# Turning a token tile round by a float32 product instead of by DMA, and placing the transform's groups anew

## The chip, the cores and the metric

The program runs on one core of a Trainium2 chip. The metric is the device time of one execution in microseconds (us), as the median of several runs. Besides, one execution was recorded by the hardware profiler; the rows below are from that one. The engines are TensorE (PE, with its weight loads as PEld), VectorE (DVE), ScalarE (ACT), GpSimd (POOL) and SyncE, whose queue (SP) issues most of the DMA transfers. Each engine works through its own instructions in order and waits on semaphores for the others. A tile is a buffer of 128 partitions; a bank is a tile of 128x512 float32 values in PSUM, the memory into which TensorE writes.

## The reference, cut to what matters

Two batches of 768 tokens go through three layers: a retention attention, then a Fourier mixing with an MLP, then a second MLP. The change lies in the Fourier mixing of the second batch.

```python
X = np.fft.fft(x, axis=1)          # along 768 tokens
X = np.fft.fft(X, axis=2)          # along 512 features
u = x + np.real(X)
un = (u - mean(u)) / np.sqrt(var(u) + 1e-6)
x = u + np.maximum(un @ w_ch1, 0.0) @ w_ch2
# and then the second MLP layer on that x
```

## The kernel before

**What is computed where.** A batch `b` is held as six token tiles `U[b][0..5]` of 128x512. The token transform uses the symmetry of cosine and sine: tile `m` and tile `3 + m`, which holds the mirrored tokens, are added and subtracted, and the same is done along the features. `fold_half` does this for one `m` (lines 528 to 545) and leaves a folded tile `f` (`folds[b, m][2]`). For the second batch (`b` = 1) the fold goes one step further: the folded tile of `m` = 2, with its token order reversed, is added to and subtracted from the folded tile of `m` = 0. The reversed tile is called `turned`, the two results `radd` and `rsub` (lines 588 to 594). Each is split into a float16 part and a float16 remainder (`fadd`, `fsub`, made by `pair_of_rows`: a cast on ACT, then a subtraction on POOL, lines 561 to 565). `dft1_two` (line 612) then makes the five groups of the token transform, banks `ps_d_2`, `ps_d_3`, `ps_d_4`, `ps_d_0`, `ps_d_1`, from `fm` (the fold of `m` = 1), `fadd` and `fsub`. `dft2_*` makes the feature transform from them, and the layer norm and `unT` (the transposed input of the MLP) follow.

**How the tile is turned.** `fold_turn` (lines 569 to 583) writes `f` to DRAM (`turned_d`), copies it there row by row in reversed order (`turned_e`), and loads it back as `turned`. Row 0 stays zero. That makes three DMA transfers, one behind the other on the SP queue.

**What runs meanwhile.** The MLP of the first batch (blocks 0 and 1) and later of the second (blocks 2 and 3) is a long list of steps. Step `n` does the up product of one slice `f` of the hidden layer (line 843, bank `ps_h`, 12 matmuls 128x384; from block 2 on also in a form with fewer products, line 952), its ReLU on ACT and the remainder on DVE (lines 857 and 858), and the down product of the slice of three steps before (line 1003, banks `ps_y`, 9 matmuls 128x512). At the end of a block DVE adds the three banks `ps_y` to `u` (line 1109, the drain), which frees them for the next block.

**What sets the order.** `put(n, task)` hangs the second batch's work into step `n` (lines 1453 to 1468). The tile framework then orders each engine's instructions by these priorities and by a timeline that it simulates itself, so the order on an engine is fixed before the run. `fold_turn` stands at step 20, `fold_mid` and `fold_both` at 22, the five groups at 22.5, 23, 23.5, 24 and 24.5. Banks come from three rings: `at` (three, for attention, the weights' conversion, the transform), `dn` (three, for `ps_y`) and `up` (two, for `ps_h`).

Of the kernel before, what the change touches and what calls it, by code (L numbers as in the profile page):

```python
# [11 lines left out]
F32 = mybir.dt.float32  # L12
# [7 lines left out]
P = 128  # L20
B, H, S, D = 2, 8, 768, 64
DM, DF = 512, 2048
# [29 lines left out]
EARLY0, GATEN, B1, SPC, DS, DC, DFO, DD, D1S, D2S, AO, YA, NR, NE, LN1, L1, L2, F01, F02, TL, R1, R2, SE, PR1, LAG, UB, FB, NW, MQ, SPL = 11, 8, 6, 2.0, 2.0, 5, 1.0, 0.5, 0.5, 1.0, "aba", "aa", 2, 0, 3, 2.5, 2.5, 16, 4, 3, 1.5, 2, "dddd_dppp", 0, 3, 3, 13, 11, 1, 3  # L52
# [22 lines left out]
def split16(a):  # L75
    hi = a.astype(np.float16)
    lo = (a - hi.astype(np.float64)).astype(np.float16)
    return hi, lo


def shape_tables():
    t = np.arange(TB)
    s = np.arange(NS)
    ang = 2.0 * np.pi * ((t[:, None] * s[None, :]) % S) / S
    cs = np.cos(ang) * TS
    sn = np.sin(ang) * TS
    d = np.arange(P)
    dd = np.arange(ND)
    cd = np.cos(2.0 * np.pi * ((d[:, None] * dd[None, :]) % DM) / DM) * TS
    dse, dso = d[:, None] * dd[None, 2:-1:2], (d[:, None] + 1) * dd[None, 1::2]  # L90
    sd = np.sin(2.0 * np.pi * (np.concatenate([dso, dse], 1) % DM) / DM) * TS
    sd[P - 1, :P] *= 0.5

    def lay(a, n):
        parts = [x.reshape(n, P, -1).transpose(1, 0, 2) for x in split16(a)]
        return np.ascontiguousarray(np.stack(parts, 1))

    def full(a, n):
        return np.ascontiguousarray(a.astype(np.float32).reshape(n, P, -1).transpose(1, 0, 2))

    even, odd = np.arange(0, DM, 2), np.arange(1, DM, 2)
    wide = np.stack([np.cos(2.0 * np.pi * (d[:, None] * even % DM) / DM), np.cos(2.0 * np.pi * (d[:, None] * odd % DM) / DM),
                     -np.sin(2.0 * np.pi * (d[:, None] * even % DM) / DM), -np.sin(2.0 * np.pi * ((d[:, None] + 1) * odd % DM) / DM)], 1) * TS
    wide[0, 2] = np.where(even % 4, -0.5, 0.5) * TS
    wide[P - 1, 3] *= 0.5
    so = np.concatenate([np.arange(0, NT, 2), np.arange(1, NT, 2)])
    tc = np.cos(2.0 * np.pi * (t[:2 * P, None] * so % S) / S) * TS
    ss = so[so < TB]
    ts = np.sin(2.0 * np.pi * (t[:2 * P, None] * ss % S) / S) * TS
    ts[0] = np.sin(2.0 * np.pi * (2 * P * ss % S) / S) * TS  # L110
    r3 = np.round(2.0 * np.cos(2.0 * np.pi * (2 * P * so % S) / S)) / 2
    cr4 = np.stack([np.where(so % 2, -2.0, 0.0)] * 2 + [r3] * 2) * TS

    def two(a, n):
        return np.ascontiguousarray(np.stack([x.reshape(2, P, n).transpose(1, 0, 2) for x in split16(a)], 1))

    n = np.arange(P)
    expo = np.zeros((P, H + 8 + P), np.float32)
    expo[:, :H] = n[:, None]
    expo[:, H:H + 4] = P  # L120
    for i, m in enumerate((n < D, n >= D, n > 0, n == 0)):
        expo[:, H + 4 + i] = m
    expo[:, H + 8:] = np.eye(P)
    return {
        "cs2": two(tc, NT),
        "sn2": two(ts, TB),
        "cr4": cr4.astype(np.float16),
        "cs": lay(cs, 3),
        "sn": lay(sn[:, :TB], 3),
        "cd": lay(np.concatenate([cd[:, ::2], cd[:, 1::2]], 1), 1)[:, :, 0],  # L130
        "sd": lay(sd, 1)[:, :, 0],
        "cr": ((np.where(s % 2, -1.0, 1.0) - 1.0) * TS).astype(np.float16)[None],
        "dr": np.tile(np.where(dd[::2] % 4, -0.5, 0.5) * TS, (2, 1)).astype(np.float16),
        "cs32": full(cs, 3),
        "sn32": full(sn[:, :TB], 3),
        "wide": wide.astype(np.float32),
        "expo": expo,
    }
# [3 lines left out]
def tile_retention_fourier_mlp(ctx: ExitStack, tc: tile.TileContext, a: dict, out: bass.AP):  # L142
    nc = tc.nc
    pe, act, dve, pool, sp = nc.tensor, nc.scalar, nc.vector, nc.gpsimd, nc.sync

    const = ctx.enter_context(tc.tile_pool(name="const", bufs=1))
# [10 lines left out]
    dram = ctx.enter_context(tc.tile_pool(name="dram", bufs=1, space=DRAM))  # L157
# [5 lines left out]
    def bank(which, name):  # L163
        return banks[which].tile([P, 512], F32, tag=which, name=name)

    def f32t(name, spare=None):
        if spare is not None:
            return wpool.tile([P, 512], F32, tag=f"w2_{spare}", name=name)
        return fp.tile([P, 512], F32, tag="f", name=name)
# [12 lines left out]
    man.__enter__()  # L182
    lamb = const.tile([P, H], F32, name="lamb")
    sp.dma_start(lamb, a["lam"].partition_broadcast(P))
    expo = const.tile([P, H + 8 + P], F32, name="expo")
    act.dma_start(expo, a["expo"])
    upper, lower, nonzero, zero = (expo[:, H + 4 + i:H + 5 + i] for i in range(4))
    ident = expo[:, H + 8:]

    loaded = {}  # L190

# [93 lines left out]
    def run(steps):  # L285
        for t in steps:
            pass
        return t
# [237 lines left out]
    folds = {}  # L526
# [29 lines left out]
    def fold_two(m):  # L556
        run(fold_half(1, m, 1, pool))
        run(fold_half(1, m, 0))
        return folds[1, m][2]

    def pair_of_rows(f, name):
        t = hl(name)
        act.copy(t[:, 0], f)
        pool.tensor_tensor(t[:, 1], f, t[:, 0], op=ALU.subtract)
        return t

    turned = {}

    def fold_turn():
        f = fold_two(2)  # L570
        t = f32t("r256").bitcast(F16)[0:1].rearrange("p (two n) -> p two n", two=2)[:, :, :ND]
        act.copy(t[:, 0], f[0:1, :ND])
        pool.tensor_tensor(t[:, 1], f[0:1, :ND], t[:, 0], op=ALU.subtract)
        sp.dma_start(rows4[1][2:4], t)
        z = turned["f"] = f32t("turned")
        pool.memset(z[0:1], 0.0)
        d, e = (dram.tile([P, DM], F32, name=f"turned_{x}") for x in "de")
        sp.dma_start(d, f)
        x_, y_ = d[:], e[:]
        halves_of = [[DM // 2, 2], [DM, P - 1], [1, DM // 2]]  # L580
        sp.dma_start(bass.AP(y_.tensor, y_.offset + DM, halves_of),
                     bass.AP(x_.tensor, x_.offset + (P - 1) * DM, [[DM // 2, 2], [-DM, P - 1], [1, DM // 2]]))
        sp.dma_start(z[1:P], e[1:P])

    def fold_mid():
        fhl[1, 1] = pair_of_rows(fold_two(1), "fm1")

    def fold_both():
        f, z = fold_two(0), turned["f"]
        act.copy(f[0:1, ND:], folds[1, 2][2][0:1, ND:])  # L590
        for nm, op in (("add", ALU.add), ("sub", ALU.subtract)):
            r = f32t(f"r{nm}1")
            dve.tensor_tensor(r, f, z, op=op)
            fhl[1, nm] = pair_of_rows(r, f"f{nm}1")
# [17 lines left out]
    def dft1_two(g, bk):  # L612
        c0, w, tn, _ = GRP[g]
        cos = tn == "cs"
        n = NT // 2 if cos else HB
        t = tab[tn + "2"]
        ps = bank(bk["d"], f"ps_d1_{g}")
        todo = [(1, slice(0, 2 * n), 1), ("add" if cos else "sub", slice(0, n), 0), ("sub" if cos else "add", slice(n, 2 * n), 0)]
        if w > 1:
            for nm, o, m in todo:  # L620
                for i, (x, y) in enumerate(PASS):
                    pe.matmul(ps[:w, o], fhl[1, nm][:, x, c0:c0 + w], t[:, y, m, o], start=nm == 1 and i == 0,
                              stop=not cos and nm == "add" and i == 2, skip_group_check=True)
        else:
            for y in range(2):
                for nm, o, m in todo:
                    pe.matmul(ps[:2 - y, o], fhl[1, nm][:, :2 - y, c0], t[:, y, m, o], start=nm == 1 and y == 0, stop=False,
                              skip_group_check=True)
        if cos:
            pe.matmul(ps[:w, :2 * n], rows4[1][:, c0:c0 + w], tab["cr4"], start=False, stop=True, skip_group_check=True)  # L630
        w = max(w, 2)
        t = cst[1, g] = csp.tile([P, 2, NT], F16, tag=f"cs{g}", name=f"cst1_{g}")
        hi, lo = (t[:w, x, :2 * n].rearrange("p (i e) -> p e i", e=2) for x in range(2))
        z = ps[:w, :2 * n].rearrange("p (e i) -> p e i", e=2)
        act.activation(hi, z, AF.Copy, scale=CS)
        dve.scalar_tensor_tensor(lo, z, CS, hi, op0=ALU.mult, op1=ALU.subtract)
# [682 lines left out]
    bk1 = {"a": "at", "s": "at", "i": "at", "o": "at", "st": "at", "d": "at", "l": "at", "p": "at"}  # L1319
# [110 lines left out]
    def put(n, task):  # L1430
        bg.setdefault(max(int(n), 0), []).append((n, len(bg), task))
# [26 lines left out]
    n = t + DC + DFO  # L1458
# [2 lines left out]
    put(n, fold_both)  # L1461
    n += DD
    for i, g in enumerate((2, 3, 4, 0, 1)):
        put(n + i * D1S, lambda g=g: dft1_two(g, bk1))
    n += 4 * D1S + 1
    for j in range(3):
        put(n + j * D2S, lambda j=j: (run(dft2_q(1, j, bk1)), run(sub_sin(1, j)), dft2_x(1, j), ln_a(0, 2, j)))
# [99 lines left out]
```

## Time and profile before

| what | value |
|---|---|
| median of 3 runs | 589.98 us (589.07 to 590.15) |
| the profiled execution | 588.64 us, span 586.9 us |
| PE busy | 561.4 us (96% of the span) |
| DVE, POOL, ACT busy | 403.9, 335.5, 302.7 us |
| mean granted TensorE clock | 0.994 |

The span is the time from the first to the last instruction in the record; the execution's own time is 1.7 us longer. PE is busy nearly throughout, so what counts is where it isn't, and what it waits for there. [...]

### The profile page before, as it was taken

What the parts mean: (1) busy time and instruction counts of PE and PEld (TensorE: products, weight loads), DVE (VectorE), ACT (ScalarE), POOL (GpSimd) and SP (SyncE); (2) the same over time, 40 slices, a digit from 0 to 9 for tenths busy, and PEclk for the clock granted to TensorE, in tenths of its full rate; (3) what the DMA queues carried; (4) which work ended last, traced back from release to release, by engine and by line L of the source; (5) the groups of instructions that cost most, each with busy time, mean ns of one, the idle gap of its engine ahead of it and who ended that gap; (6) DMA issues with size and microseconds to landing.
All of it is one profiled execution on the core that took longest, in us unless ns stands there. A gap on an engine that the chain in (4) does not pass through costs nothing.

```text
span 586.9 us, 12192 instructions
## 1 busy us (share of the span) xinstructions
PE 561.4 (96%) x4700; PEld 384.5 (66%) x4700; DVE 403.9 (69%) x917; ACT 302.7 (52%) x621; POOL 335.5 (57%) x355
## 2 busy tenths in 40 slices
PE   7979999999995999989999899999999999999997
PEld 4746555566552554666677677776777778878885
DVE  6897896787864447888687866557656665756544
ACT  4867888733232232645688788954243454322320
POOL 7826599976442353655367678764096676223511
PEclk9999999999997999999999999999999999999999
DMA  8997089950010010244265443510120125002101
GB/s 282 407 412 278 23 274 252 330 182 3 1 43 12 1 36 20 58 111 152 73 166 181 144 162 115 167 27 1 55 55 1 18 88 59 1 1 75 37 1 55
DMA packets 47417, 63.92 MB, mean 109 GB/s; under 512 B 26236, under 2 KB 29183, under 8 KB 47358
## 3 DMA queue, kind: packets, MB, share of 16 engines
q1 hardware_dynamic: 46542, 62.92, 34.6%
q8 instruction: 37, 0.61, 0.4%
q10 hardware_dynamic: 816, 0.21, 0.2%
q14 instruction: 22, 0.18, 0.1%
HBM read 52.63 MB, written 6.81 MB: 101 GB/s over the span
## 4 chain that ended last, share of the span: by engine, by line
PE 62%; DVE 13%; ACT 8%; POOL 6%; DMA 6%; issue 5%; SPq 0%; DVEq 0%; POOLq 0%; ACTq 0%
PE ps_y L1003 25%; PE ps L952 21%; PE ps_h L843 5%; DVE wr L876 2%; DMA turned<-turned_e 2%; PE ps_y L1050 2%; POOL m L393 1%; DMA turned_e<-turned_d 1%; PE ps_a L1050 1%; PE ps_b L1050 1%; POOL w L343 1%; PE ps_s L381 1%; ACT top L324 1%; ACT w L341 1%; DMA ws<-in_w 1%
## 5 line engine op out<-in xcount | busy, mean ns | idle before, releaser
L1003 PE MATMUL ps_y<-w,h 128*128 128x512 f16 (+1 forms) x1026 | 249.4, 378 | 2.7 <-DVE h L989 1.6
L1003 PEld LDWEIGHTS <-h 128*128 128x128 f16 x1032 | 98.0, 98 | 89.5 <-ACT h L988 2.7
L952 PEld LDWEIGHTS <-sw 128*128 128x128 f16 x1104 | 94.6, 98 | 21.7 <-issue 3.3
L952 PE MATMUL ps<-th,sw 128*128 128x192 f16 x756 | 86.0, 246 | 2.1 <-DVE s L969 1.2
L343 POOL TENSOR_TENSOR w<-wf,w 128x512 f16<-128x512 f32 x58 | 66.9, 1160 | 32.3 <-ACT w L341 32.2
L952 PEld LDWEIGHTS <-w 128*128 128x128 f16 x828 | 70.9, 98 | 11.0 <-issue 0.8
L843 PE MATMUL ps_h<-unT,w 128*128 128x384 f16 x396 | 72.8, 328 | 1.8 <-DVE h L858 1.7
L952 PE MATMUL ps<-unT,w 128*128 128x192 f16 x552 | 61.6, 246 | 0.0
L843 PEld LDWEIGHTS <-w 128*128 128x128 f16 x396 | 38.0, 98 | 30.7 <-issue 3.2
L888 POOL TENSOR_TENSOR sw<-ws,sw 128x512 f16<-128x512 f32 x32 | 36.9, 1167 | 18.4 <-ACT sw L887 18.3
L341 ACT CAST w<-wf 128x512 f16<-128x512 f32 x58 | 35.1, 611 | 10.1 <-DVE wf L328 7.2
L1238 ACT ACTIVATE h<-ps 128x384 f16<-128x384 f32 x44 | 21.7, 496 | 34.6 <-DVE ps L1245 30.0
L917 POOL TENSOR_TENSOR th<-ts,th 128x384 f16<-128x384 f32 x22 | 20.2, 936 | 27.1 <-ACT th L916 27.1
L318 DVE SCALAR_TENSOR_TENSOR wf<-ws,ps_w 128x512 int32<-128x512 int32 x34 | 23.2, 684 | 17.1 <-ACT ps_w L316 6.7
L393 POOL TENSOR_TENSOR m<-m,m 128x512 f16<-128x512 f32 x24 | 31.6, 1332 | 5.6 <-ACT m L391 3.6
L785 POOL TENSOR_TENSOR rs<-rs,neghalf 128x1 f32<-128x1 f32 x24 | 13.5, 567 | 34.8 <-DVE rs L783 34.8
L1267 POOL TENSOR_TENSOR hh<-s,hh 128x256 f16<-128x256 f32 x22 | 14.4, 677 | 32.9 <-ACT hh L1266 30.9
L806 POOL TENSOR_TENSOR uns<-un,uns 128x512 f16<-128x512 f32 x21 | 25.4, 1207 | 13.5 <-ACT uns L805 13.5
L988 ACT ACTIVATE h<-ps 128x384 f16<-128x384 f32 x48 | 22.4, 487 | 20.5 <-DVE ps L982 18.6
L989 DVE SCALAR_TENSOR_TENSOR h<-ps,h 128x384 f16<-128x384 f32 x48 | 25.4, 553 | 10.6 <-ACT h L988 10.0
L857 ACT ACTIVATE h<-ps_h 128x384 f16<-128x384 f32 x36 | 17.1, 482 | 25.7 <-PE ps_h L843 25.7
L952 PE MATMUL ps<-unT,sw 128*128 128x192 f16 x276 | 30.3, 246 | 0.0
(248 smaller groups left out, 1031.5 us busy)
## 6 DMA issues: line engine op xcount, KB each, us to landing
ws<-in_w SPq DMA_DIRECT2D x25, 511.8 KB, 6.3
ws<-in_w2b SPq DMA_DIRECT2D x16, 511.8 KB, 4.3
ws<-in_w1b SPq DMA_DIRECT2D x16, 511.8 KB, 3.9
kt<-in_kt SPq DMA_DIRECT2D x12, 256.0 KB, 3.6
qt<-in_qt SPq DMA_DIRECT2D x12, 256.0 KB, 4.9
v<-in_v SPq DMA_DIRECT2D x12, 256.0 KB
k<-in_k SPq DMA_DIRECT2D x12, 256.0 KB, 5.0
pre<-in_w SPq DMA_DIRECT2D x4, 511.8 KB, 6.9
```

The costliest lines, as they stand in the source:

```text
L318: dve.scalar_tensor_tensor(ti, raw[:, :, 0], 13, part.bitcast(I32), op0=ALU.logical_shift_right, op1=ALU.bitwise_or)
L341: act.copy(hi, t)
L343: gate["lo"] = pool.tensor_tensor(lo, t, hi, op=ALU.subtract)
L393: pool.tensor_tensor(t[:, 1], m32, t[:, 0], op=ALU.subtract)
L806: pool.tensor_tensor(s_[:, 1], un, s_[:, 0], op=ALU.subtract)
L843: pe.matmul(ps, w[:, i, k, fo:fo + P], x[:, j, k, :], start=n == 0, stop=n == 11)
L888: pool.tensor_tensor(lo, z, hi, op=ALU.subtract)
L952: pe.matmul(ps, lhs, rhs, start=start and n == 0, stop=n == 5, skip_group_check=True)
L988: gate["relu"] = act.activation(hi, z, AF.Relu)
L989: dve.scalar_tensor_tensor(lo, z, 0.0, hi, op0=ALU.max, op1=ALU.subtract)
L1003: pe.matmul(ps, h[:, x, j * P:(j + 1) * P], w[:, y, c], start=f == first and n == 0, stop=f == NF - 1 and n == 2, skip_group_check=True)
L1050: pe.matmul(ps[:, c], lhs[:, x], rhs[:, y], start=start == 1 and n == 0 and p == 0, stop=n == 2, skip_group_check=True)
```

## The change

The tile is no longer turned by DMA. `fold_turn` makes a 128x128 tile `turning` on POOL: the identity of `expo` read from its last column backwards, with one added zero column. `fold_both` multiplies it with `f` in one float32 product into a bank of the `at` ring (`ps_turned`), and DVE reads that bank for `radd` and `rsub`. The groups are put at `n + 1 + i * D1S / 2`, which is 23.5, 23.75, 24, 24.25 and 24.5.

```diff
-    expo = np.zeros((P, H + 8 + P), np.float32)
+    expo = np.zeros((P, H + 8 + P + 1), np.float32)
...
-    expo[:, H + 8:] = np.eye(P)
+    expo[:, H + 8:-1] = np.eye(P)
...
-        z = turned["f"] = f32t("turned")
-        pool.memset(z[0:1], 0.0)
-        d, e = (dram.tile([P, DM], F32, name=f"turned_{x}") for x in "de")
-        sp.dma_start(d, f)
-        x_, y_ = d[:], e[:]
-        halves_of = [[DM // 2, 2], [DM, P - 1], [1, DM // 2]]
-        sp.dma_start(bass.AP(y_.tensor, y_.offset + DM, halves_of),
-                     bass.AP(x_.tensor, x_.offset + (P - 1) * DM, [[DM // 2, 2], [-DM, P - 1], [1, DM // 2]]))
-        sp.dma_start(z[1:P], e[1:P])
+        turned["p"] = f32t("turning")[:, :P]
+        pool.tensor_copy(turned["p"], expo[:, H + 8 + P:H + 8:-1])
...
     def fold_both():
-        f, z = fold_two(0), turned["f"]
+        z = bank(bk1["d"], "ps_turned")
+        pe.matmul(z, turned["p"], folds[1, 2][2], start=True, stop=True)
+        f = fold_two(0)
...
-        put(n + i * D1S, lambda g=g: dft1_two(g, bk1))
+        put(n + 1 + i * D1S / 2, lambda g=g: dft1_two(g, bk1))
```

Lines behind the changed function stand five lower in the changed kernel (line 1003 there is 998, 858 is 853, 1109 is 1104). The order of instructions differs from PE's row for `ps_turned` to somewhat behind the start of block 2, and nowhere later. Three places:

**The new product.** On PE, in the changed kernel, it stands between the up product of slice 6 of block 1 (`ps_h_1_6`) and the down product of slice 3 (`w_0_3`).

```order
L838 MATMUL ps_h_1_6_2508<-unT_1_1188,w_0_1_1038 128x384
L583 MATMUL ps_turned<-f_2_2400,turning 128x512
L998 LDWEIGHTS h_1_1_2230
L998 MATMUL ps_y_1_0_2370<-w_0_3_1112,h_1_1_2230 128x512
L998 LDWEIGHTS h_1_1_2230
L998 MATMUL ps_y_1_0_2370<-w_0_3_1112,h_1_1_2230 128x512
```

Before, the row of `ps_turned` was not there and its neighbours followed on each other.

**The first products that need the turned tile.** On PE, in the down product of slice 6 (`w_0_6`). Before:

```order
L1003 LDWEIGHTS h_1_3_2526
L1003 MATMUL ps_y_1_2_2372<-w_0_6_1269,h_1_3_2526 128x512
L622 LDWEIGHTS fsub_2562
L622 MATMUL ps_d_2_2565<-sn_1_1922,fsub_2562 128x192
L622 LDWEIGHTS fsub_2562
L622 MATMUL ps_d_2_2565<-sn_1_1922,fsub_2562 128x192
```

And in the changed kernel:

```order
L998 LDWEIGHTS h_1_3_2521
L998 MATMUL ps_y_1_0_2370<-w_0_6_1269,h_1_3_2521 128x512
L617 LDWEIGHTS fsub_2559
L617 MATMUL ps_d_2_2586<-sn_1_1922,fsub_2559 128x192
L617 LDWEIGHTS fsub_2559
L617 MATMUL ps_d_2_2586<-sn_1_1922,fsub_2559 128x192
L617 LDWEIGHTS fsub_2559
L617 MATMUL ps_d_3_2599<-sn_1_1922,fsub_2559 128x192
```

They stood behind eight of the nine matmuls of that down product, and now stand behind three of them.

**The start of block 2.** On DVE, between the drain of block 1 and the first remainder of block 2 (`h_2_0`, which frees the first `ps_h` bank). `bst` are statistics for the layer norm, `tr` and `ts` sums over `unT`. Before, the three drains of line 1109 stood directly ahead of three `BN_STATS` and these rows:

```order
L899 TENSOR_TENSOR tr_2_0_3006<-unT_2_2774 128x384
L899 TENSOR_TENSOR tr_2_2_3008<-unT_2_2774 128x384
L780 BN_AGGR mv_3_2_3413<-bst_3_2_3411 128x2
L780 BN_AGGR mv_0_0_3844<-bst_0_0_3842 128x2
L780 BN_AGGR mv_0_1_3884<-bst_0_1_3882 128x2
L920 TENSOR_TENSOR ts_0_2_0_3010<-tr_2_0_3006 128x192
L858 SCALAR_TENSOR_TENSOR h_2_0_3044<-ps_h_2_0_3031,h_2_0_3044 128x384
```

In the changed kernel only the first drain stands ahead of the `BN_STATS` and the two `tr`; the other two follow those, then the `BN_AGGR`, and then:

```order
L915 TENSOR_TENSOR ts_0_2_0_3007<-tr_2_0_3003 128x192
L778 TENSOR_SCALAR rs_3_2_3412<-mv_3_2_3410 128x1
L772 BN_STATS bst_0_2_3945<-u_119 128x6
L772 BN_STATS bst_1_0_4916<-u_119 128x6
L853 SCALAR_TENSOR_TENSOR h_2_0_3041<-ps_h_2_0_3028,h_2_0_3041 128x384
```

Two further `BN_STATS` have moved ahead of the remainder.

## Rows read from the trace of the kernel before

**Rows 1.** PE's waits over the whole span: total us, times, longest us.

```profile
PE ps_d L622 <- ACT fsub L563: 6.5, 1, 6.5
```

**Rows 2.** The chain of waits, 160 to 187 us: start us, us, what.

```profile
160.83 1.98 DMA turned_d<-f
162.83 7.99 DMA turned_e<-turned_d
170.84 12.32 DMA turned<-turned_e
183.25 0.70 DVE radd L593
183.97 0.63 ACT fadd L563
184.67 1.50 POOL fadd L564
```

**Rows 3.** Windows: length, PE, PEld, DVE, ACT, POOL busy, granted clock, DMA share, GB/s.

```profile
178.85:185.31 6.46, 0.01 (x2) 0.01 (x1) 2.06 (x4) 1.29 (x3) 0.64 (x1) 0.79 0.04 16
185.31:190.31 5.00, 4.92 (x23) 2.62 (x23) 4.21 (x6) 1.94 (x5) 3.32 (x3) 0.58 0.00 0
190.31:240.00 49.69, 49.69 (x303) 26.76 (x303) 29.35 (x72) 16.19 (x41) 22.06 (x30) 1.00 0.08 17
240.00:335.00 95.00, 90.42 (x743) 63.86 (x740) 75.30 (x170) 62.95 (x126) 57.37 (x57) 1.00 0.45 133
```

**Rows 4.** The window from the clock's fall to its return.

```profile
183.00:189.50 6.50, 4.11 (x18) 2.31 (x18) 6.18 (x9) 2.42 (x5) 3.15 (x3) 0.50 0.00 0
```

**Rows 5.** PE's timeline at full clock: start us, us, instructions merged.

```profile
162.00 2.11 PE L843 MATMUL ps_h<-unT,w 128*128 128x384 f16 x12
163.95 2.11 PE L1003 MATMUL ps_y<-w,h 128*128 128x512 f16 x9
165.89 2.11 PE L843 MATMUL ps_h<-unT,w 128*128 128x384 f16 x12
...
246.44 0.66 PE L952 MATMUL ps<-unT,sw 128*128 128x192 f16 x6
246.94 0.66 PE L952 MATMUL ps<-th,sw 128*128 128x192 f16 x6
```

**Rows 6.** PE's timeline, float32 products (two records each).

```profile
38.36 1.45 PE L602 MATMUL ps_d<-sn,f 128*128 128x384 f32 x4
...
47.88 3.29 PE L718 MATMUL ps_pq<-wide,cst 128*128 128x256 f32 x14
```

**Rows 7.** Timelines of DVE, ACT, POOL and SP around the folds.

```profile
160.53 0.28 DVE L544 TENSOR_TENSOR f<-o 128x128 f32<-128x128 f32 x1
...
162.71 0.69 DVE L470 SCALAR_TENSOR_TENSOR u<-ps_o,int 128x512 f32<-128x512 f32 x1
...
173.13 0.28 DVE L544 TENSOR_TENSOR f<-o 128x128 f32<-128x128 f32 x1
...
173.44 0.40 ACT L590 COPY f<-f 1x255 f32<-1x255 f32 x1 [1.02 <-DVE f L544]
...
155.62 0.52 POOL L576 MEMSET turned<- 1x512 f32 x1
...
207.63 35.11 SPq L808 DMA_TRANSPOSE unT<-uns  x7
```

**Rows 8.** Timelines of DVE and PE at the start of block 2.

```profile
225.16 1.89 DVE L1109 SCALAR_TENSOR_TENSOR u<-ps_y,u 128x512 f32<-128x512 f32 x3 [2.35 <-PE ps_y L1003]
226.97 1.87 DVE L777 BATCH_NORM_STATS2 bst<-u 128x6 f32<-128x512 f32 x3
...
230.15 0.55 DVE L858 SCALAR_TENSOR_TENSOR h<-ps_h,h 128x384 f16<-128x384 f32 x1
...
225.69 4.07 PE L843 MATMUL ps_h<-unT,w 128*128 128x384 f16 x24
...
231.01 2.11 PE L843 MATMUL ps_h<-unT,w 128*128 128x384 f16 x12
```

More of the change, by code (lines that the diff above doesn't have):

```diff
@@ L184, in tile_retention_fourier_mlp @@
     sp.dma_start(lamb, a["lam"].partition_broadcast(P))
-    expo = const.tile([P, H + 8 + P], F32, name="expo")
+    expo = const.tile([P, H + 8 + P + 1], F32, name="expo")
     act.dma_start(expo, a["expo"])
     upper, lower, nonzero, zero = (expo[:, H + 4 + i:H + 5 + i] for i in range(4))
-    ident = expo[:, H + 8:]
+    ident = expo[:, H + 8:H + 8 + P]
     loaded = {}
```

## The prediction

> **What bounds the kernel now.** PE is the bound nearly everywhere, so I first read PE's waits over the whole span. One stands out: 6.5 us for the group products of line 622, released by the cast `fsub` [rows 1]. The chain of waits shows what is behind that cast: `f` is written to DRAM at 160.83, reversed there by 170.82, and is back as `turned` only at 183.16, 22.3 us after it left; then come `radd`, the cast, the remainder [rows 2]. The windows show the cost on PE: nothing from 178.85 to 185.31, and afterwards a granted clock that is 0.58 in the mean over the next 5.00 us [rows 3]. [...] So PE pays twice: it stands still, and then it works at half speed. From 190.31 to 240 it is busy without a gap at full clock [rows 3].
>
> **The loss, worked out.** Between 178.85 and 190.31, 6.46 + 5.00 = 11.46 us, PE does 23 matmuls (the window's count): by the order 16 with 192 or 193 columns, 2 with 386, 4 with 384, 1 with 512. At full clock six of 192 columns take 246.94 - 246.44 = 0.50 us (0.083 each), twelve of 384 take 163.95 - 162.00 = 1.95 (0.1625 each), nine of 512 take 165.89 - 163.95 = 1.94 (0.216 each) [rows 5]. So the work is 16 x 0.083 + 2 x 0.166 + 4 x 0.1625 + 0.216 = 2.53 us, and the loss is 11.46 - 2.53 = 8.93 us: 6.46 of standing still, 2.47 of slow clock, with some waiting for the remainder of `fadd` in it.
>
> **What becomes of the wait.** The new product stands on PE where the trace shows 163.95, the start of the down product of slice 3 [rows 5]. It needs three things. `f` is complete at 160.53 + 0.28 = 160.81, 3.1 us ahead. The tile `turning` takes the place of the memset at 155.62 (0.52 us) on POOL [rows 7]; a copy of 128x128 there should cost between that and the 1.50 us of a 128x512 subtraction [rows 2]. POOL has until 163.95, so this costs nothing; without that cover it would be at most 1 us. The bank comes free from the attention's last chunk, whose last reader is the DVE row at 162.71, done at 163.40, 0.55 us ahead [rows 7]. So PE shouldn't wait.
>
> `radd` then no longer waits for DMA, but for the fold of `m` = 0 (173.13 + 0.28 = 173.41) and the ACT copy of its row 0 (until 173.84) [rows 7]. With 0.70 each for `radd` and `rsub`, 0.63 for a cast and 1.50 for a remainder [rows 2], the cast of `fsub` is done at about 175.9 and its remainder at about 178.3. PE gets to the first `fsub` product later than that: from 163.95 on it has the new product (0.95, below), three down and three up products (3 x 1.94 + 3 x 1.95), seven products of `fm` (7 x 0.163) and three more down matmuls (0.65), which gives 178.36. The margin is 2.5 us for the cast; the remainder is needed another 1.5 us later. So no part of the wait is left. The words "a step later" mislead: in the order shown, the first `fsub` product stands behind three matmuls of that down product instead of eight. The new positions only keep the groups from blocking PE; they bring nothing of their own.
>
> **What is added.** One float32 product of 128x512. No such shape is in the trace. Two of 384 columns take 1.45 us, seven of 256 take 3.29 [rows 6]: 0.725 and 0.47 each, 0.255 per 128 columns, so 0.98 for 512; I take 0.95, since a row's last product overlaps what follows. The lower bound is the float16 price, 0.216, the upper one twice a 384-column product, 1.45. It lies bare on PE, since PE has no gap there.
>
> The three DMAs that go are the SP queue's only work of that stretch; what follows on SP are the transposes from 207.63 on [rows 7], so nothing moves up behind them. `radd` and `rsub` now read a bank; the row at 162.71 reads a bank of the same size in 0.69, as `radd` does from SBUF in 0.70 [rows 2, 7], so that costs nothing.
>
> **A new wait at block 2.** Before, block 2's first up products start at 225.69; DVE drains block 1 from 225.16 (1.89 for three) and does three statistics (1.87), and the remainder of `h_2_0` begins at 230.15 [rows 8]. PE's third up product (231.01) needs the bank which that frees by about 230.6: a slack of 0.4. In the changed order two more statistics (2 x 0.62 = 1.25) stand ahead of the remainder, while the first drain can start some 0.65 earlier (its three matmuls now stand ahead of the other six). Remainder later by 0.6, less the slack, plus a semaphore: an estimate of 0.45 us of new wait, between 0 and the 1.25 less 0.1. I take 0.45. Queued behind that product on PE are the whole down products of block 2.
>
> **The sum.** -8.93 + 0.95 + 0.45 = -7.53 us. Against the profiled execution's 588.64 (span 586.9 and 1.7 around it) that gives 581.1. The median of the runs shown is 1.34 higher, so the prediction is 589.98 - 7.53 = 582.4.
>
> **The clock's part, weighed.** Rows 3 and 4 show the clock at 0.50 after a gap of PE and at 1.00 wherever it had none. If the slow stretch came from something else and stayed, the gain would be 6.46 - 0.95 - 0.45 = 5.06, and the time 584.9. [...]
>
> **The rivals.**
> *More is given back between 225 and 265* (583.5 to 585.5). The stretch from 240 to 335 has PE gaps of 95.00 - 90.42 = 4.6 us in all, with DVE busy 75.30 and ACT 62.95 [rows 3]: engines that take turns with PE, so a reordering of a few instructions shifts small waits there. If the full 1.15 at block 2 falls due and another 1 to 2 us behind it, the gain is 4.5 to 6.5. For it: the changed order puts drains behind statistics. Against it: the remainders of the later slices don't all come later.
> *The gain vanishes in that stretch* (589, no change). If DVE, ACT and POOL worked off a backlog there that doesn't depend on PE, the 7.5 us would come back as waits. Against it: at 225.16 DVE had just stood 2.35 us waiting for PE's `ps_y` [rows 8], so what it does from there on moves with PE. A part of it (to 587) is possible.
> *PE itself waits at the head of its queue* (slower, 591 or more). The new product blocks all PE work behind it, where before only DVE waited for the turned tile. If `f` or the bank came late by L, PE would lose L, and about 2.5 us of slow clock again if L is like the gap of today. The change is slower once L exceeds 7.5, or some 5 with the slow clock. That would put `f` at 169 or later instead of 160.81; against it stands its 3.1 us of margin. The bank's 0.55 is thin, but what is late there is one short DVE read.
> *The change doesn't do what it says*: the DMAs are gone from SP's order, so this is out, apart from the "step later" above.
>
> **Chances and range.** Forecast (581.3 to 583.5) 0.62; more given back (583.5 to 585.5) 0.20; a large part lost in the later stretch (585.5 to 588.8) 0.06; no change 0.06; slower 0.04; better than 581.3, if the small waits from 240 on shrink, 0.02. The range 580.7 to 585.6 holds the first two and the last, 0.84. The measurement tells apart about 0.2%, 1.2 us: faster 0.90, same 0.06, slower 0.04.
>
> **What the profile after would show.** PE's wait at line 622 gone, and no stretch under clock 1.00 near 180 to 190; a float32 `ps_turned` of about 0.95 us without idle time ahead of it; `radd` about 10 us earlier, released by ACT or DVE; a new PE wait of 0.2 to 1 us at the third up product of block 2; the gaps from 240 to 335 at about 4.6 us still. Wrong would be: a PE wait at `ps_turned`, a wait of some us at `fsub`, or gaps after 240 that grow by several us.

## The result and the profile after

The changed kernel takes **579.85 us** in the median of four runs (579.60 to 580.52), the kernel before, run beside it, 589.86 (589.07 to 590.15): a ratio of 0.9834 with a 95% interval of 0.9817 to 0.9851, so 10 us faster. The prediction was 582.4 with a range from 580.7 to 585.6: the sign was right, the time lies 0.85 us below the range. The profiled execution took 580.52 us, its span is 578.7 and the mean granted clock 0.999, as a share of full speed. That is the slowest of its four runs, and the profiled execution of before (588.64) lies below all of the runs beside it, so the two profiles differ by 8.1 us only; 1.9 us of the 10 lie between executions and in no row.

PE's waits from 160 to 345 us of the changed kernel (total us, times, longest us):

```profile
PE ps_y L998 <- ACT h L983: 1.1, 2, 0.8
PE ps L947 <- DVE wf L318: 0.7, 1, 0.7
PE ps L947 <- DVE s L964: 0.7, 1, 0.7
PE ps_h L838 <- DVE h L853: 0.4, 1, 0.4
```

The wait of 6.5 us for `fsub` [rows 1] is gone. So are two that the prediction didn't look at one by one, which the view of the kernel before has for the same stretch:

```profile
PE ps_y L1003 <- DVE h L989: 1.6, 1, 1.6
...
PE ps L952 <- DVE t L976: 0.4, 1, 0.4
```

PE's timeline around the fold and at the start of block 2 (start us, us, instructions merged, in brackets the idle time before them):

```profile
162.59 2.11 PE L838 MATMUL ps_h<-unT,w 128*128 128x384 f16 x12
164.54 1.02 PE L583 MATMUL ps_turned<-f,turning 128*128 128x512 f32 x2
165.40 2.11 PE L998 MATMUL ps_y<-w,h 128*128 128x512 f16 x9
...
179.06 0.49 PE L617 MATMUL ps_d<-sn,fsub 128*128 128x192 f16 x4
...
218.43 4.06 PE L838 MATMUL ps_h<-unT,w 128*128 128x384 f16 x24
...
224.16 2.11 PE L838 MATMUL ps_h<-unT,w 128*128 128x384 f16 x12 [0.38 <-DVE h L853]
```

The product stands between two rows without idle time and holds PE from 164.54 to 165.40, 0.86 us. The first `fsub` product comes at 179.06 with no wait ahead of it. Block 2 begins at 218.43, where it was 225.69 [rows 8]. Its third up product now waits 0.38 us.

Windows of the changed kernel (length, PE, PEld, DVE, ACT and POOL busy, granted clock, DMA share, GB/s):

```profile
178.85:185.31 6.46, 6.46 (x43) 3.55 (x42) 3.72 (x9) 3.50 (x7) 2.27 (x2) 1.00 0.00 0
185.31:190.31 5.00, 5.00 (x38) 3.02 (x37) 1.69 (x4) 1.52 (x4) 0.27 (x1) 1.00 0.00 0
190.31:240.00 49.69, 49.30 (x321) 28.18 (x320) 31.43 (x82) 17.91 (x42) 26.64 (x33) 1.00 0.16 33
232.00:327.00 95.00, 92.29 (x755) 64.91 (x753) 74.55 (x171) 63.61 (x128) 57.83 (x57) 1.00 0.48 134
240.00:335.00 95.00, 92.30 (x743) 64.14 (x742) 73.24 (x166) 64.34 (x129) 60.28 (x60) 1.00 0.47 137
```

Beside [rows 3]: where PE stood still and then ran at half clock, it is now busy at full clock. And the stretch from 240 to 335, or the same work 8 us earlier, has 2.7 us of PE gaps instead of 4.6. That is what the prediction did not have.

**Where the difference of the two profiles comes from**, read off at the same instruction in each. Up product 6 starts 0.59 us later (162.59 for 162.00) [rows 5], in a part of the program that is the same. From there to block 2's first up product the change gives 225.69 - 218.43 + 0.59 = 7.85 us, and loses 0.41 up to the third (231.01 for 224.16). From the third to the row of `th` products at 255.19 before and 246.20 after it gives another 2.14. Behind that 0.8 us are lost, 0.5 between 320 and 330 of the kernel before and 0.3 at the very end. 0.59 - 7.85 + 0.41 - 2.14 + 0.8 = -8.2, the difference of the spans.

### The profile page after: what moved, and what is told of

Same layout as the page of the kernel before. It is cut to its first block, busy times and chain, and to the rows that moved or that the text cites. A ratio compares the mean times of both kernels' runs of the same rounds, so it can differ in the third digit from the quotient of the medians.

```text
span 578.7 us, 12188 instructions
## 1 busy us (share of the span) xinstructions
PE 559.8 (97%) x4702; PEld 384.1 (66%) x4702; DVE 402.5 (70%) x917; ACT 302.5 (52%) x621; POOL 335.6 (58%) x355
## 4 chain that ended last, share of the span: by engine, by line
PE 43%; DVE 4%; issue 3%; POOL 3%; ACT 3%; POOLq 0%; ACTq 0%
PE ps L947 20%; PE ps_y L998 18%; PE ps_y L1045 2%; PE ps_b L1045 1%; PE ps_a L1045 1%; POOL w L343 1%; DVE tr L894 1%; DVE wf L318 1%; ACT h L983 0%; ACT half L315 0%; DVE ts L915 0%; POOL sw L883 0%; ACT wf L340 0%; ACT ps_w L316 0%; ACT th L911 0%
## 5 line engine op out<-in xcount | busy, mean ns | idle before, releaser
L343 POOL TENSOR_TENSOR w<-wf,w 128x512 f16<-128x512 f32 x58 | 66.9, 1161 | 33.1 <-ACT w L341 33.1
L838 PE MATMUL ps_h<-unT,w 128*128 128x384 f16 x396 | 71.6, 326 | 2.0 <-DVE h L853 1.8
L1262 POOL TENSOR_TENSOR hh<-s,hh 128x256 f16<-128x256 f32 x22 | 14.4, 677 | 32.9 <-ACT hh L1261 30.9
L801 POOL TENSOR_TENSOR uns<-un,uns 128x512 f16<-128x512 f32 x21 | 25.4, 1208 | 12.3 <-ACT uns L800 12.3
```

What stands on the lines that cost most here:

```text
L343: gate["lo"] = pool.tensor_tensor(lo, t, hi, op=ALU.subtract)
L801: pool.tensor_tensor(s_[:, 1], un, s_[:, 0], op=ALU.subtract)
L838: pe.matmul(ps, w[:, i, k, fo:fo + P], x[:, j, k, :], start=n == 0, stop=n == 11)
```

## The experiments

Each was timed beside the kernel before on one chip, whose median there was 588.9 to 589.1 us (9 to 17 runs each time), against 589.98 in the runs on which the prediction was built. The batches ran on different chips; as the kernel before is within 0.2 us on all of them, medians of different batches are compared below. "Row for row" means that the start of the same instruction is compared in two profiles.

### e1: the changed kernel with the groups at their old places

```diff
-        put(n + 1 + i * D1S / 2, lambda g=g: dft1_two(g, bk1))
+        put(n + i * D1S, lambda g=g: dft1_two(g, bk1))
```

> The changed kernel with the groups put back to their old positions (n + i * D1S). Theory: the new positions do nothing, since the order of every engine comes out row for row the same; 579.9 us, the wait of about 0.4 us at the third up product of block 2 again, and PE's gaps from 225 to 265 as small as in the changed kernel. Rival: the groups' new positions bring part of the gain; then 581 us or more.

Measured: 579.72 us (578.77 to 580.99), ratio 0.9843 [0.9827, 0.9859]. Row for row, every engine has the same program as in the changed kernel: the second half of the change does nothing. So this is also a second profile of the changed program, and it is used as such below.

### e4: turned by DMA still, but every transfer with 128 rows

The zero row is written to DRAM too, so the reversal and the load move 128 rows instead of 127. There is no product and no new position; PE, DVE, ACT and POOL have the order of the kernel before.

```diff
-        d, e = (dram.tile([P, DM], F32, name=f"turned_{x}") for x in "de")
-        sp.dma_start(d, f)
+        d = dram.tile([P + 1, DM], F32, name="turned_d")
+        e = dram.tile([P, DM], F32, name="turned_e")
+        sp.dma_start(d[P:P + 1], z[0:1])
+        sp.dma_start(d[:P], f)
...
-        sp.dma_start(z[1:P], e[1:P])
+        sp.dma_start(z, e)
```

> The kernel before, the tile still turned by DMA, but in whole 128 rows (row 0 comes from a zero row in DRAM) instead of 127 rows; order on all engines but SP as before. Theory A: 127 rows go through few of the DMA engines (the share was 0.06 to 0.09 while they ran), 128 rows are spread; each of the three transfers takes 2 to 3 us, the tile is there at about 169, before the other fold (173.4). Then PE's wait and the slow clock are gone without any product, 8.9 us: 581.0 us if the two small PE waits of 0.45 and 1.58 us before 252 stay, because they belong to the old order; 578.9 us if they go, because they came from the stall. Rival B: the time of a transfer lies in the reversal and the DRAM, not in the row count; then the wait stays and the time is 588 to 590.

Measured: 580.81 us (580.28 to 581.17), ratio 0.9859 [0.9847, 0.9872]; beside it before had 589.04. The last load, issued at 171.97, lets `radd` start at 175.51; before, the load alone took 12.32 [rows 2]. PE has no wait at the group products and keeps its clock:

```profile
178.00:190.00 12.00, 12.00 (x82) 6.80 (x81) 6.48 (x12) 4.76 (x11) 4.25 (x4) 1.00 0.00 0
```

So without the stall the old program is 8.2 us faster in the median. The reversal took 8.2 us, not 2 to 3 as expected; the load made the difference, as e5 shows.

Row for row the loss can be read off, since PE has the same order in both. The first group products with `fsub`, and where the same 23 matmuls end at the next row of up products, in the kernel before:

```profile
185.31 0.82 PE L622 MATMUL ps_d<-sn,fsub 128*128 128x192 f16 x4 [6.45 <-ACT fsub L563]
...
190.31 1.47 PE L843 MATMUL ps_h<-unT,w 128*128 128x384 f16 x8
```

And in e4:

```profile
179.63 0.49 PE L623 MATMUL ps_d<-sn,fsub 128*128 128x192 f16 x4
...
182.63 1.47 PE L844 MATMUL ps_h<-unT,w 128*128 128x384 f16 x8
```

The 23 matmuls take 3.00 us at full clock, where the prediction had worked out 2.53, and 5.00 in the kernel before. With the last matmul ahead of the gap (178.47 before, 179.42 in e4) the whole stretch takes 11.84 and 3.21 us: the loss is 8.63, and the term of 8.93 was 0.3 too large.

And the waits of 0.45 and 1.58 behind block 2 are still there (rows further down): they belong to the order of the old program, not to the stall.

### e5: e4 with a last load of 127 rows

```diff
-        sp.dma_start(z, e)
+        sp.dma_start(z[1:P], e[1:P])
```

> As the run with 128 rows, but the last transfer loads only 127 rows, as before; same order. It takes about 12 us again, so the tile arrives at 177 to 179, and PE waits 1 to 3 us for the cast and the remainder instead of 6.5. Theory A: the clock falls only after a long gap, so it stays at 1.00: 581.0 + 2.5 = 583.5 us (582.5 to 584.5). Rival B: any wait at this place brings the slow clock: 585.5 us or more.

Measured: 589.15 us (587.86 to 590.71), ratio 1.0001 [0.9989, 1.0013], as the kernel before. It was meant to make a short gap, because the reversal was expected to get quicker by its 128th row; it didn't (7.92 us, below), so the stall came back whole. What it shows is that one row of 128 in the last load decides over 8.3 us. The chain of waits of e5 (start us, us, what):

```profile
161.05 2.00 DMA turned_d<-f
163.10 7.92 DMA turned_e<-turned_d
171.04 12.34 DMA turned<-turned_e
183.47 0.70 DVE radd L594
```

### e6: the kernel before with one more copy of the same form

```diff
+        g = dram.tile([P, DM], F32, name="turned_g")
+        v_ = g[:]
+        sp.dma_start(bass.AP(v_.tensor, v_.offset + DM, halves_of), bass.AP(y_.tensor, y_.offset + DM, halves_of))
-        sp.dma_start(z[1:P], e[1:P])
+        sp.dma_start(z[1:P], g[1:P])
```

> The kernel before with one more copy of the turned tile inside DRAM, 8 us as the first such copy; same order otherwise. Theory A: the wait is on the path one for one and the slow clock costs a fixed 2.5 us after the gap, however long it is: 589.9 + 8.0 = 597.9 us, a PE wait of 14.5 us. Rival B: the work at half speed grows with the gap: 600 us or more. Rival C: a part is hidden later: 595 us or less.

Measured: 597.0 us (595.86 to 599.4), ratio 1.014 [1.0121, 1.016]. The copy took 7.78 us and PE waited 14.4 for `fsub`. The loss of 8.0 is the copy's own time: with the tile late, each us of it is a us of the kernel. In this profile, of the slowest of its four runs, the 23 matmuls behind the gap took 5.57 us, so the low clock cost 0.57 more than in the profile of the kernel before.

### e7 and e8: short gaps

e4 with one (e7) or two (e8) straight copies DRAM to DRAM ahead of the load, to find out whether a short gap costs the clock as well.

```diff
+        g = dram.tile([P, DM], F32, name="turned_g")
+        sp.dma_start(g, e)
-        sp.dma_start(z, e)
+        sp.dma_start(z, g)
```

> The kernel of e4 (all hops with 128 rows, 580.8) with one more copy between the reversal and the load, DRAM to DRAM, same rows in the same order. The copy should take 2 to 3.5 us (the store of the same 256 KB took 2.0, the load 3.5); of that about 1.1 us is slack (the load of e5 landed 7.5 us later than that of e4 and TensorE waited 6.4), so TensorE waits 1 to 2.5 us before the difference's first product. Theory D (a short gap keeps the clock at 2.4 GHz): 581.8 to 583.3. Rival C (any gap here is followed by the low clock, which cost 2.5 before): 584.3 to 585.8. Rival: the copy takes 8 us like the reversed one, which was then not slow for its reversal: 589.

Measured: 581.44 us (580.99 to 581.77), 0.63 above e4. A straight copy took 3.4 us. Two waits of 0.40 and 0.34 us are left on PE, with the clock at 1.00 throughout (the views give it as a share; no trace shows the 2.4 GHz): the low clock did not follow these waits, and the loss is the waiting. The time lies below both expected ranges because PE waited 0.74 us and not 1 to 2.5.

> As e7 with two such copies, 4 to 7 us more than e4 in all, of which TensorE waits 3 to 6. Theory D, clock kept: 583.8 to 586.8; the low clock behind the gap: 2.5 more, 586.3 to 589.3. With e7 and e6 it shows from which length of the wait on the granted clock falls.

Measured: 586.25 us (584.27 to 587.75), 5.44 above e4. PE waited 3.41 us and the clock fell. Windows of e8: the gap, the stretch behind it, the one after that:

```profile
178.44:181.85 3.41, 0.00 (x1) 0.01 (x1) 2.06 (x4) 1.29 (x3) 0.64 (x1) 1.00 0.15 54
181.85:185.40 3.55, 3.37 (x15) 1.83 (x16) 3.48 (x5) 0.49 (x2) 2.41 (x2) 0.52 0.00 0
185.40:190.00 4.60, 4.60 (x29) 2.36 (x28) 2.83 (x6) 2.85 (x6) 2.28 (x2) 1.00 0.00 0
```

Row for row against e4, PE loses 3.58 us up to the first `fsub` product (3.41 of it the wait), and the 23 matmuls take 4.71 us instead of 3.00, of which 0.18 is a wait for a remainder: 5.29 of the 5.44. The median alone would have fitted the theory that the clock is kept (583.8 to 586.8); the windows show that it wasn't. So the clock's part of the loss is real and a price of its own, and it is not fixed: the same matmuls took 4.57 us in e5 (behind 6.42 of waiting), 5.00 in the kernel before (6.45) and 5.57 in e6 (14.40).

### e10, e14 and e9: one pair of additions a step later

The waits of 0.45 and 1.58 that the changed kernel lost were what was left to explain. Ahead of the remainder `h` for which the down products of block 2 wait (the expectation of e9 says block 3, whose work begins later), DVE has two additions `wr` (128x512, both inputs in SBUF). The edit moves that pair behind the remainder, in e4 (e10), in the kernel before (e14) and in the changed one (e9). It doesn't move the pair alone: PE's order changes in 20 places of the 43 us behind it.

```diff
-SUMS = {(1, 0): 16, (1, 1): 18, (2, 0): 20, (2, 1): 25, (3, 0): 35, (3, 1): 38, (0, 0): 41, (0, 1): 43}
+SUMS = {(1, 0): 16, (1, 1): 18, (2, 0): 20, (2, 1): 25, (3, 0): 35, (3, 1): 39, (0, 0): 41, (0, 1): 43}
```

> The same edit in e4, whose program has the order of the kernel before and whose profile shows the wait of 1.58 us. Theory: the wait goes and with it 1.0 to 1.6 us, 579.2 to 579.8; then what the changed kernel gained beyond the prediction is the place of this pair and no part of the turned tile. Rival (the order elsewhere gave it): the wait stays or is met later, 580.5 to 581.1.

Measured: 579.36 us (579.19 to 579.92), ratio 0.9836 [0.9824, 0.9849], 1.45 below e4. The wait of 1.58 is gone; the one of 0.45 stayed. But another has grown from 0.6 us and a new one has come in:

```profile
PE ps L953 <- DVE s L970: 1.2, 1, 1.2
...
PE ps L953 <- DVE ps L978: 0.4, 1, 0.4
```

So PE's waits from 160 to 345 add up to 3.9 us instead of 4.4. Row for row, PE is 0.24 us ahead of e4 where the edit begins and 1.24 from 330 on: the edit gives 1.0 us in the profiles.

> The kernel before with nothing changed but the sums of group 3, second half, entered at 39 for 38, as in e10; its programs on TensorE, VectorE, ScalarE and GpSimd are then e10's row for row. Theory: the wait of 1.58 us goes, the wait of 6.5 us stays, 587.2 to 588.0, ratio 0.997 to 0.9985: the gain that was not predicted is to be had without the turned tile. Rival (it needs the earlier start of block 2): 588.6 to 589.9, ratio 1.000.

Measured: 587.59 us (586.47 to 588.93), ratio 0.9979 [0.9969, 0.9990], 1.49 below the kernel before beside it, with the long wait for `fsub` still there (7.1 us). Row for row the edit gives 0.76 us here (0.69 ahead where it begins, 1.45 from 330 on). So 0.8 to 1.5 us are to be had without the turned tile, by the place of the pair and the order that follows from it.

> The changed kernel with the sums of group 3, second half, entered one step later (39 for 38): VectorE then has the pair of additions wr behind the remainder h that the down products of block 3 wait for. Theory (the wait of 0 to 1.58 us there is the pair, held up by GpSimd's cast beside it): that wait is 0 in every execution, and the time is 579.0 to 579.9 (the changed kernel 579.85, its copy with the old group positions 579.72 with a wait of 0.88 in its profile). Rival (the wait has another cause): the wait stays. The edit also reorders 86 rows of TensorE later on, which may cost or give some tenths.

Measured: 579.95 us (579.13 to 580.23), ratio 0.9841 [0.9828, 0.9854]. The wait is 0 in its profile, but the time is that of the changed kernel: 0.05 above the expected range, and no gain. A wait of 0.4 for `ps` and one of 0.2 for `th` have come in. What the edit saves there is little, as the changed kernel mostly had it already.

### e16: the same pair without GpSimd beside it

e4 with the float16 remainder of one tile filled with zeros instead of subtracted.

```diff
         act.copy(s_[:, 0], un)
-        pool.tensor_tensor(s_[:, 1], un, s_[:, 0], op=ALU.subtract)
+        if (m, blk, j) == (0, 3, 1):
+            pool.memset(s_[:, 1], 0.0)
+        else:
+            pool.tensor_tensor(s_[:, 1], un, s_[:, 0], op=ALU.subtract)
```

> The kernel of e4 with one operation of GpSimd taken away from beside the pair wr: the float16 remainder of one normalised tile of block 3 (128 tokens, row L807 at 240.74, 1.61 us) is filled with zeros beforehand instead of being subtracted, so that this part of the computation is left out; TensorE's order is e4's row for row. In e4 the pair takes 2.43 us, two additions that take 0.68 each where GpSimd is idle. Theory (the pair is held up by GpSimd's subtraction of two tiles): the pair takes 1.4 to 1.8 us, TensorE's wait of 1.58 behind it becomes 0.4 to 0.9, and the time is 579.7 to 580.3. Rival (it is held up by the transfers or by its own buffers): the pair takes 2.4 us again, the wait stays, 580.5 to 581.2.

Measured: 579.64 us (578.58 to 581.36), ratio 0.9837 [0.9822, 0.9851]. The pair took 1.45 us, as the theory has it, but it also started late, so the wait shrank only from 1.58 to 1.10, less than expected. Both theories hold a part. Row for row the edit gives 0.49 us. The five runs lie too far apart to read more from their median, and the profile is that of the slowest, for a reason that has nothing to do with the edit (the last section shows it).

The pair in five profiles, DVE's row and POOL's rows beside it. Before:

```profile
247.41 3.11 DVE L876 TENSOR_TENSOR wr<-w 128x512 f32<-128x512 f16 x2
...
247.25 1.16 POOL L343 TENSOR_TENSOR wst<-wf,wst 128x512 f16<-128x512 f32 x1
248.37 1.60 POOL L806 TENSOR_TENSOR uns<-un,uns 128x512 f16<-128x512 f32 x1
```

e4, with the wait behind it on PE:

```profile
240.47 2.43 DVE L877 TENSOR_TENSOR wr<-w 128x512 f32<-128x512 f16 x2 [0.59 <-DMA unT<-uns]
...
240.74 1.61 POOL L807 TENSOR_TENSOR uns<-un,uns 128x512 f16<-128x512 f32 x1
...
243.48 0.39 PE L1004 MATMUL ps_y<-w,h 128*128 128x512 f16 x1 [1.58 <-DVE h L990]
```

e16:

```profile
241.66 1.45 DVE L880 TENSOR_TENSOR wr<-w 128x512 f32<-128x512 f16 x2 [1.08 <-DMA unT<-uns]
...
240.81 1.15 POOL L343 TENSOR_TENSOR wst<-wf,wst 128x512 f16<-128x512 f32 x1
```

The changed kernel:

```profile
240.14 1.40 DVE L871 TENSOR_TENSOR wr<-w 128x512 f32<-128x512 f16 x2
...
239.22 1.16 POOL L343 TENSOR_TENSOR wst<-wf,wst 128x512 f16<-128x512 f32 x1
240.84 1.71 POOL L801 TENSOR_TENSOR uns<-un,uns 128x512 f16<-128x512 f32 x1 [0.46 <-ACT uns L800]
```

e1, the same program once more:

```profile
239.70 2.41 DVE L871 TENSOR_TENSOR wr<-w 128x512 f32<-128x512 f16 x2
...
240.40 1.16 POOL L801 TENSOR_TENSOR uns<-un,uns 128x512 f16<-128x512 f32 x1 [0.44 <-ACT uns L800]
```

The pair took 1.28 us where POOL stood idle beside all but its last 0.42 us (e10, from 243.52), and a subtraction of 128x512 on POOL takes 1.16 in the mean (58 at L343 of the kernel before). Where the two met, the pair, the subtraction or both took longer: in the changed kernel's profile POOL's took 1.71 and DVE's pair 1.40; in e1's, which is the same program, POOL's took 1.16, the pair 2.41, and PE waited 0.88 at 242.69; in e4 they took 1.61 and 2.43. In the kernel before both additions met a subtraction (3.11). Why, no run shows. Besides, the pair waits in e4 and e16, by its releaser for a transposing transfer that still reads the buffer (0.59 and 1.08 us). Where that transfer stands is set on the SP queue. In e4, with the old order, a weight load goes between the two transposes of a tile:

```profile
233.92 1.19 SPq L809 DMA_TRANSPOSE unT<-uns  x1
235.21 1.47 SPq L277 DMA_DIRECT2D ws<-in_w2b  x1
236.77 1.19 SPq L809 DMA_TRANSPOSE unT<-uns  x1
```

In the changed kernel both go ahead of it, and DVE doesn't wait for the buffer:

```profile
233.35 2.50 SPq L803 DMA_TRANSPOSE unT<-uns  x2
235.94 1.50 SPq L277 DMA_DIRECT2D ws<-in_w2b  x1
```

That the order of these two is why the buffer is free in time is read from the rows; no run changed it alone.

The other wait, of 0.45 for `t`, went for a plainer reason. Before, PE had nothing to do there:

```profile
245.95 0.66 PE L952 MATMUL ps<-th,w 128*128 128x192 f16 x6 [0.45 <-DVE t L976]
```

In the changed kernel two down matmuls stand in that place:

```profile
238.06 0.59 PE L998 MATMUL ps_y<-w,h 128*128 128x512 f16 x2
238.67 0.66 PE L947 MATMUL ps<-th,w 128*128 128x192 f16 x6
```

### e11 and e13: the price of the product

e11 makes the product three times, e13 in two float16 products (with the pair moved as in e9).

```diff
...
-        pe.matmul(z, turned["p"], folds[1, 2][2], start=True, stop=True)
+        for x in range(2):
+            pe.matmul(z, turned["p"], turned["f"][:, x], start=x == 0, stop=x == 1)
```

> The changed kernel with its reversal product made three times into the same bank (the first two are written over). The profile of the changed kernel has one at 0.86 us from its start to the next row's, with TensorE never idle from 160 to 220. Theory A (the product lies on the path): two more cost 1.7 us, 581.1 to 582.0. Rival B (they are taken up by waits further on, those of 0.4 to 0.9 us at 224, 242, 255 and 271): 579.6 to 580.6. The order later changes in some places too.

Measured: 583.99 us (582.42 to 584.38), 4.1 above the changed kernel where 1.3 to 2.2 were expected. In its profile the three products start at 163.97, 164.83 and 165.69, 0.86 apart with no idle time between them; row for row the two more put PE back by 1.71 us. That execution, the fastest of the six, has a span 1.9 above the changed kernel's. It also has a wait for ACT's `h` that is longer than in any other kernel:

```profile
243.80 0.60 PE L1000 MATMUL ps_y<-w,h 128*128 128x512 f16 x2 [1.96 <-ACT h L985]
```

The order of all engines behind the products is another one here, so the whole time doesn't isolate their price. Its median lies another 1.6 us above that execution: the two runs with a mean granted clock of 1.000 took 582.42 and 582.94 us, the four with 0.994 to 0.997 took 583.90 to 584.38, so the clock had fallen in those; where, no trace shows. The price is taken from the rows: 0.86.

> The changed kernel with the pair's sums a step later (as in e9) and with the reversal made by two float16 products, of the tile's rounded half and of its remainder, in place of the one in float32; one cast on ScalarE and one subtraction on GpSimd more, at a place where TensorE waits for neither. A float16 product of 512 columns takes 0.22 us, so the two take 0.43 to 0.44 against 0.86. Theory A: 0.42 less than e9, 579.2 to 579.8. Rival B: TensorE waits for the remainder, and the reversal costs as much as before or more, 580 to 581.

Measured: 579.41 us (579.01 to 580.05), ratio 0.9839 [0.9821, 0.9856], 0.54 below e9 in the median, with 0.42 expected; the two products hold PE from 164.18 to 164.61, 0.43 us. It has the lowest median of the kernels that turn the tile on PE, but the intervals of all of them overlap, and so does that of e10: no version is shown to beat the changed kernel.

## Why the prediction was wrong in its size

- **The loss of 8.93 us** was right in kind and 0.3 us too large. The stall is gone, none of the changed kernel's windows shown is under clock 1.00, and block 2 starts 7.85 us earlier, with 7.98 predicted for loss and product together. e4 and e5 give 8.2 and 8.3 in the median for the stall by itself, and the rows of e4 8.63. The sum took each of the 23 matmuls at its price in a long row of like ones, 2.53 us; they take 3.00, as e4's rows show some 0.09 us more at each of five places where the next matmul belongs to another product. So the slow clock cost 2.0 us and not 2.47.
- **The clock's part** was right: it was 0.50 from 183.00 to 189.50 in the kernel before [rows 4], with a gap of 6.46 us, and 0.52 behind 3.41 us of waiting (e8); it was 1.00 without the gap (e4, the changed kernel) and with waits of 0.40 and 0.34 (e7). The case in which the slow stretch stays, 584.9, is excluded. What sets the clock, no run shows.
- **The product**: 0.86 measured for 0.95, bare on PE and without a wait ahead of it, as said. `turning` took POOL 0.28 us, less than either bound, at no cost. `radd` starts at 174.05, 9.2 us earlier; the cast of `fsub` is done at 175.99 and its remainder at 178.18, for 175.9 and 178.3.
- **The new wait at block 2**: 0.38 at the third up product, for 0.45.
- **"They bring nothing of their own"**, of the new positions, is right. That they keep the groups from blocking PE, said beside it, is not: e1 shows that they don't even change the order.
- **The step that failed** is what the prediction made of the stretch from 225 on. It took a changed order there as a risk alone ("more is given back between 225 and 265", 0.20; a gain there, 0.02) and expected the gaps from 240 on "at about 4.6 us still". They shrank to 2.7, and 2.14 us were gained between 231 and 255. The old order's waits of 0.45 and 1.58 were in the profile before, and the changed order's transposes on SP and its casts on ACT stood in the order that could be read; the prediction did not set the two beside each other. e10 and e14 put 0.8 to 1.0 us by the rows, 1.5 by the medians, on the place of one pair of additions and the order that follows from it. In the changed kernel the pair stays where it was and what stands beside it has moved; that this is why its wait was shorter is read from rows, and e1 shows that even in the new program part of it comes and goes from one execution to the next.
- **The base** was off too. The sum was added to the median of three runs, 589.98; over the 9 to 17 runs beside each experiment the kernel before has 588.9 to 589.1. By these the forecast would have been 581.5, and the change is worth 9.2 us. The rows from up product 6 to the end give 7.85 - 0.41 + 2.14 - 0.8 = 8.8, where the sum had 7.53: the 2.14 and the 0.8 are in no term of it. Of the 2.55 us between 582.4 and 579.85 the rows so hold 1.3 and the base 0.9; the other 0.3 lie within the scatter of the runs.

## What to carry to other kernels

An edit that makes a scheduler order anew is costed in both directions: list the waits that the profile shows behind the edit, and look up for each whether its waiting and its releasing instruction still stand in that order. Before a transfer is replaced by computing, look at what it takes per byte beside its neighbours: here one row more in the last load (e4 against e5) gave 8.3 of the 9.2 us with no product at all. And the time to which a sum is added needs more than three runs when the effect that it leaves out is 1 us.

## What the runs showed of the hardware

**A transfer's time hung on its row count and form.** 256 KB (254 with 127 rows) took 2.0 us into DRAM as 128 rows (the kernel before, e5, e6), 3.0 to 3.6 as a straight copy of 128 rows DRAM to DRAM (e7, e8), and 2.6 to 3.5 as a load of 128 rows, up to `radd` (e4, e7, e8, e10); as 2x127x256 or 2x128x256 it took 7.8 to 8.2, reversed or not (e4 to e6), and as a load of 127 rows 12.3 (the kernel before, e5, e6). Windows from 172 to 175 us, during the last load, in e4 (128 rows) and in e5 (127):

```profile
172.00:175.00 3.00, 3.00 (x18) 1.47 (x15) 2.70 (x8) 0.90 (x2) 0.00 (x0) 1.00 0.38 93
```

```profile
172.00:175.00 3.00, 3.00 (x16) 1.35 (x15) 2.03 (x6) 0.90 (x2) 0.00 (x0) 1.00 0.08 24
```

The share of the 16 DMA engines that were busy is 0.38 against 0.08, which is 6 and 1.3 engines in the mean of the window. In the kernel before it was 0.34 over the 2.0 us of the store, 0.09 over the 7.99 of the reversal and 0.06 over the 12.32 of the load: the longer the transfer, the smaller the share. That e4 and e5 lie so far apart with one row of 128 between them is measured; what sets the number of engines, no run shows.

**The clock fell at another place too, in some executions.** At about 104 us, where no edit reaches, PE waits for DVE's `h` (1.07 us in the changed kernel, 1.30 in the kernel before). In e16's profile the granted clock fell behind it, to 0.62 in the mean from 105 to 109; in e4's, with the same order, it stayed at 1.00. e16's row and window (columns as in the windows above), then e4's:

```profile
104.15 3.28 PE L847 MATMUL ps_h<-unT,w 128*128 128x384 f16 x11 [1.14 <-DVE h L862]
...
105.00:109.00 4.00, 4.00 (x15) 1.68 (x14) 3.64 (x6) 2.71 (x6) 2.55 (x3) 0.62 1.07 401
```

```profile
104.62 1.14 PE L844 MATMUL ps_h<-unT,w 128*128 128x384 f16 x6 [1.24 <-DVE h L859]
...
105.00:109.00 4.00, 3.62 (x21) 1.85 (x20) 3.44 (x6) 2.71 (x6) 2.46 (x3) 1.00 1.05 396
```

Row for row it cost 1.2 us. e6's profile (mean clock 0.982, its long gap included) has the same behind a wait of 1.74 us at 104.18; the kernel before has 1.00 behind 1.30, the changed one 1.00 behind 1.07. So the length of the wait by itself didn't decide it here, and one execution can be about a us longer than another for this alone.

**One program, two waits.** In two executions of one program the pair on DVE took 1.40 and 2.41 us, and PE's wait behind it was 0 and 0.88: a wait in one profile is not by itself a property of the program.
